# Block-sparse attention and a multiplicative FFN on one core: transposed scores in packed TensorE tiles, x kept on chip, w3 folded into w_out, the FFN interleaved with attention

## The chip, the cores and the metric

The kernel runs on one core of one Trainium2 chip. The metric is the device time of one execution in microseconds (us), as a median of several executions. Every run had runs of the kernel before as company on the same chip; the rounds ran on several chips, on which the kernel before had medians of 515.2 to 516.3 us, so times of different rounds are compared too. A run over 1.5% above the fastest of its kernel counts as slow, and verdicts use the others, called fast. Ratios are the mean time of one kernel's fast runs over that of the other's in the same rounds, so they are not quite the ratio of the medians.

Engines: PE is TensorE (matmuls; PEld is its weight load), ACT is ScalarE, DVE is VectorE, POOL is GpSimd, SP is SyncE. PSUM is the memory that matmuls write to.

## The reference, cut to what matters

```python
# q, k, v: (4 batches, 8 heads, 768 tokens, 64); blocks of 32 tokens
scores = q @ k.T / 8
mask   = near diagonal | first/last block row or column | 3 sampled blocks per block row
attn   = softmax(where(mask, scores, -1e9));  out = attn @ v
x = out.transpose(0, 2, 1, 3).reshape(3072, 512)     # heads side by side
a = x @ w1;  b = x @ w2                              # 512 -> 1024
h = (a * b) @ w3                                     # 1024 -> 1024
y = h @ w_out                                        # 1024 -> 512, float32
```

Nothing stands between `@ w3` and `@ w_out`, so `w3 @ w_out` can be formed once.

## The kernel before

Attention runs first, for each of 32 heads; x goes to DRAM in bf16; then the FFN reads it back transposed. The mask is part of the score matmul: Q and K carry 24 extra rows (64 + 24 = 88), which add -400 to masked scores. A column of ones in V gives the softmax sum.

```python
AUG = D + NB                                            # 88 rows
QTaugs = [aug_pool.tile([AUG, S], BF16, ...) for i in range(4)]
KTaugs = [aug_pool.tile([AUG, S], BF16, ...) for i in range(4)]
# ...
for c in range(NKC):                                    # 6 token chunks
    tq = tr_ps.tile([D, 128], BF16, tag="trq")
    nc.tensor.transpose(tq, qb16[:, c, :], ident)       # 64 rows of output
    nc.vector.tensor_copy(QTaug[:D, c * 128:(c + 1) * 128], tq)
    tk = tr_ps.tile([D, 128], BF16, tag="trq")
    nc.tensor.transpose(tk, kb16[:, c, :], ident)
    nc.vector.tensor_copy(KTaug[:D, c * 128:(c + 1) * 128], tk)
for kc in range(NKC):
    Sps = s_ps_pool.tile([128, S], F32, tag="sps")
    lhs = KTaug[:, kc * 128:(kc + 1) * 128]
    nc.tensor.matmul(Sps[:, 0:512], lhsT=lhs, rhs=QTaug[:, 0:512], start=True, stop=True)
    nc.tensor.matmul(Sps[:, 512:768], lhsT=lhs, rhs=QTaug[:, 512:768], start=True, stop=True)
    E = asb2.tile([128, S], BF16, tag="E")
    nc.scalar.activation(E, Sps, AF.Exp, scale=1.0 / 8.0)
    for qs in range(NKC):
        nc.tensor.matmul(Ops[:, qs, :], lhsT=E[:, qs * 128:(qs + 1) * 128],
                         rhs=Vaug[:, kc, :], ...)       # 65 columns
# ... normalize, nc.sync.dma_start(out=xd[b, h], in_=ox)
for t in range(NTT):                                    # FFN, 512 tokens each
    # xT by transposing DMA; pa = x w1, pb = x w2; hT = pa * pb
    # pg = hT w3 (384 matmuls in all); po = gT w_out; store
```

The softmax here doesn't subtract the row's maximum and nothing guards it: scores larger than these inputs give would overflow.

## Time and profile before

The median is 515.7 us. From the page of the profile: the span, the busy line, and of the 40 slices of the span the busy tenths of PE and ACT and the granted TensorE clock (PEclk), and the chain.

```profile
span 514.2 us, 7561 instructions
...
PE 490.2 (95%) x2880; PEld 223.7 (43%) x2880; DVE 138.2 (27%) x540; ACT 224.3 (44%) x313; POOL 50.8 (10%) x140
...
PE   2999999999999999999999579999999999999996
...
ACT  0465555555555555555464313333333333333332
...
PEclk9999999999999999999999999999999999999999
...
PE 95%; issue 1%; DMA 1%; DVE 1%; SPq 1%; POOL 1%; ACT 0%; POOLq 0%; ACTq 0%
```

The last line is the chain of work that ended last, by engine. PE is busy nearly all the time and is nearly all of the chain. That alone doesn't tell how fast it works. The PEclk row misleads here: the record of the granted clock has its first entry, full speed, at 305.6 us. Where there is no record yet, the page draws 9.

The timeline shows what the clock was. Columns: start (us), duration (us), engine, line, operation, output<-inputs, shapes, count. One iteration of attention:

```profile
152.33 0.51 PE L175 MATMUL Ops<-Vaug,E 128*128 128x65 bf16 x6
...
152.66 0.62 PE L168 MATMUL Sps<-QTaug_121,KTaug_125 88*128 88x512 bf16 x1
...
153.06 0.42 PE L170 MATMUL Sps<-QTaug_121,KTaug_125 88*128 88x256 bf16 x1
...
153.42 0.32 PE L157 MATMUL tq<-ident,qb_2218 128*64 128x128 bf16 x1
...
153.52 0.31 PE L160 MATMUL tk<-ident,kb_2219 128*64 128x128 bf16 x1
153.58 0.81 ACT L173 ACTIVATE E<-Sps 128x768 bf16<-128x768 f32 x1 [0.60 <-PE Sps L170]
```

The next Ops starts at 153.77: a period of 1.44 us. Read starts, not durations, since matmuls are pipelined. The 512-column score matmul keeps its successor back by 0.40 us here, 0.41 in the median of every stretch of attention. The 256 columns behind it should need 0.21 us, yet tq starts 0.35 us later: 0.14 us are lost where the output width changes. The chain that ended last (start, duration, what) shows the same matmul shape at both speeds at the beginning of the FFN:

```profile
301.51 1.71 PE pb L223 x4
303.21 1.71 PE pa L219 x4
304.92 1.27 PE pb L223 x4
306.19 0.86 PE pa L219 x4
...
316.55 13.81 PE pg L234 x64
```

Four 512-column matmuls take 1.71 us, then, after 4.7 us of uninterrupted work (from 300.9 us), 0.86 us, and 13.81 / 64 = 216 ns each from there on. So the whole attention stage ran at half the clock.

| Stage of the kernel before | From, to (us) | What sets it |
|---|---|---|
| Attention, 192 iterations | 13 to 291 | PE at half clock, 1.44 us an iteration |
| x to DRAM and back | 291 to 301 | DMA |
| FFN, 960 matmuls of 512 columns | 301 to 510 | PE at full clock, 216 ns each |

### The profile page before, as it was taken

To read this page: it belongs to the slowest core of one execution; us is meant where nothing else is said; L and a number is where in the kernel's file an instruction comes from. 1 tells how busy PE (TensorE), PEld (TensorE's weight loads), DVE (VectorE), ACT (ScalarE), POOL (GpSimd) and SP (SyncE) were. 2 spreads that over 40 slices of the span, in tenths; PEclk is the share of its full clock that TensorE was granted. 3 is DMA by queue.
4 is the path that set the end of the run, shared out by engine and by line. 5 is a ranking of instruction groups with operands and counts; after the bars stand their busy time and mean duration, and the time that the engine had idled before them with its cause. 6 is when DMAs were issued, how large, how long until landed. Compare 5 with 4: busy or idle time off the path is not lost.

```text
span 514.2 us, 7561 instructions
## 1 busy us (share of the span) xinstructions
PE 490.2 (95%) x2880; PEld 223.7 (43%) x2880; DVE 138.2 (27%) x540; ACT 224.3 (44%) x313; POOL 50.8 (10%) x140
## 2 busy tenths in 40 slices
PE   2999999999999999999999579999999999999996
PEld 1444444444444444444444224444444444444442
DVE  3323233333333323235554312021030130210300
ACT  0465555555555555555464313333333333333332
POOL 5221121212121212121100000000000000000000
PEclk9999999999999999999999999999999999999999
DMA  7453444444545353546554332111101200201002
GB/s 136 92 119 78 86 96 98 93 100 88 106 85 108 79 115 78 116 113 203 183 172 138 98 82 31 30 64 41 61 22 41 83 23 20 82 1 55 28 0 82
DMA packets 120681, 42.74 MB, mean 83 GB/s; under 512 B 114308, under 2 KB 114500, under 8 KB 120644
## 3 DMA queue, kind: packets, MB, share of 16 engines
q1 hardware_dynamic: 120644, 42.25, 34.2%
q8 instruction: 22, 0.36, 0.3%
q14 instruction: 15, 0.12, 0.1%
HBM read 29.36 MB, written 9.44 MB: 75 GB/s over the span
## 4 chain that ended last, share of the span: by engine, by line
PE 95%; issue 1%; DMA 1%; DVE 1%; SPq 1%; POOL 1%; ACT 0%; POOLq 0%; ACTq 0%
PE Ops L175 17%; PE pg L234 16%; PE Sps L168 16%; PE pb L223 8%; PE pa L219 8%; PE po L243 8%; PE Sps L170 8%; PE tq L157 8%; PE tk L160 5%; SPq L209 1%; DMA xT<-x_dram 1%; DMA x_dram<-ox 0%; ACT E L173 0%; DVE KTaug_125 L161 0%; DVE QTaug_122 L158 0%
## 5 line engine op out<-in xcount | busy, mean ns | idle before, releaser
L173 ACT ACTIVATE E<-Sps 128x768 bf16<-128x768 f32 x192 | 152.7, 810 | 135.9 <-PE Sps L170 133.4
L175 PE MATMUL Ops<-Vaug,E 128*128 128x65 bf16 x1152 | 98.5, 243 | 1.2 <-ACT E L173 1.2
L175 PEld LDWEIGHTS <-E 128*128 128x128 bf16 x1152 | 68.2, 126 | 38.2 <-issue 24.1
L234 PE MATMUL pg<-hT,w3sb 128*128 128x512 bf16 x384 | 83.9, 379 | 0.0
L228 DVE TENSOR_TENSOR hT<-pa_sb,pb 128x512 bf16<-128x512 bf16 x48 | 33.0, 688 | 164.4 <-PE pb L223 153.6
L219 PE MATMUL pa<-xT,w1sb 128*128 128x512 bf16 x192 | 51.5, 389 | 8.0 <-issue 5.8
L234 PEld LDWEIGHTS <-w3sb 128*128 128x128 bf16 x384 | 37.6, 98 | 45.3
L227 ACT CAST pa_sb<-pa 128x512 bf16<-128x512 f32 x48 | 28.1, 586 | 62.3 <-PE pa L219 62.3
L238 ACT CAST gT<-pg 128x512 bf16<-128x512 f32 x48 | 28.1, 586 | 59.9 <-PE pg L234 59.9
L223 PE MATMUL pb<-xT,w2sb 128*128 128x512 bf16 x192 | 50.6, 387 | 0.0
L243 PE MATMUL po<-woutsb,gT 128*128 128x512 bf16 x192 | 42.4, 379 | 0.0
L219 PEld LDWEIGHTS <-w1sb 128*128 128x128 bf16 x192 | 19.0, 99 | 31.2 <-issue 9.4
L223 PEld LDWEIGHTS <-w2sb 128*128 128x128 bf16 x192 | 19.1, 100 | 24.8 <-issue 3.1
L168 PE MATMUL Sps<-QTaug_122,KTaug_126 88*128 88x512 bf16 x48 | 29.7, 620 | 0.0
L168 PE MATMUL Sps<-QTaug_121,KTaug_125 88*128 88x512 bf16 x48 | 29.7, 619 | 0.0
L168 PE MATMUL Sps<-QTaug_123,KTaug_127 88*128 88x512 bf16 x48 | 29.7, 619 | 0.0
L168 PE MATMUL Sps<-QTaug_124,KTaug_128 88*128 88x512 bf16 x48 | 29.7, 619 | 0.0
L243 PEld LDWEIGHTS <-gT 128*128 128x128 bf16 x192 | 18.8, 98 | 22.7
L248 ACT COPY osb<-po 128x512 f32<-128x512 f32 x24 | 14.1, 586 | 27.4 <-PE po L243 27.4
L144 POOL CAST Vaug<-vf 128x384 bf16<-128x384 f32 x32 | 16.3, 510 | 58.3 <-issue 30.3
L170 PE MATMUL Sps<-QTaug_122,KTaug_126 88*128 88x256 bf16 x48 | 20.1, 418 | 0.0
L170 PE MATMUL Sps<-QTaug_121,KTaug_125 88*128 88x256 bf16 x48 | 19.9, 419 | 0.0
(244 smaller groups left out, 426.9 us busy)
## 6 DMA issues: line engine op xcount, KB each, us to landing
scratch<-in_moe_w_dram SPq DMA_DIRECT2D x16, 512.0 KB
qf<-in_q_dram SPq DMA_DIRECT2D x32, 192.0 KB
kf<-in_k_dram SPq DMA_DIRECT2D x32, 192.0 KB
vf<-in_v_dram SPq DMA_DIRECT2D x32, 192.0 KB
out_dram<-osb SPq DMA_DIRECT2D x24, 256.0 KB
x_dram<-ox SPq DMA_DIRECT2D x32, 96.0 KB
scratch<-in_moe_w_out_dram SPq DMA_DIRECT2D x8, 256.0 KB
xT<-x_dram SPq DMA_TRANSPOSE x24
```

The source lines that it names most:

```text
L157: nc.tensor.transpose(tq, qb16[:, c, :], ident)
L168: nc.tensor.matmul(Sps[:, 0:512], lhsT=lhs, rhs=QTaug[:, 0:512], start=True, stop=True)
L170: nc.tensor.matmul(Sps[:, 512:768], lhsT=lhs, rhs=QTaug[:, 512:768], start=True, stop=True)
L173: nc.scalar.activation(E, Sps, AF.Exp, scale=1.0 / 8.0)
L175: nc.tensor.matmul(Ops[:, qs, :], lhsT=E[:, qs * 128:(qs + 1) * 128], rhs=Vaug[:, kc, :], start=(kc == 0 and qs == 0), stop=(kc == NKC - 1 ...
L219: nc.tensor.matmul(pa, lhsT=w1_sb[:, dmc, fft * 128:(fft + 1) * 128], rhs=xT[:, dmc, :], start=(dmc == 0), stop=(dmc == NDMC - 1))
L223: nc.tensor.matmul(pb, lhsT=w2_sb[:, dmc, fft * 128:(fft + 1) * 128], rhs=xT[:, dmc, :], start=(dmc == 0), stop=(dmc == NDMC - 1))
L227: nc.scalar.copy(pa_sb, pa)
L228: nc.vector.tensor_mul(hT[:, fft, :], pa_sb, pb)
L234: nc.tensor.matmul(pg, lhsT=w3_sb[:, ffc, ff2t * 128:(ff2t + 1) * 128], rhs=hT[:, ffc, :], start=(ffc == 0), stop=(ffc == NFFC - 1))
L238: nc.scalar.copy(gT[:, ff2t, :], pg)
L243: nc.tensor.matmul(po, lhsT=gT[:, ff2c, tsub * 128:(tsub + 1) * 128], rhs=wout_sb[:, ff2c, :], start=(ff2c == 0), stop=(ff2c == NFFC - 1))
```

## The change

The kernel was rebuilt around TensorE:

- Scores come out with keys on partitions. Two heads share the array: each contracts over 64 rows, one in rows 0 to 63, one in rows 64 to 127.
- Values: the output has 32 channels on partitions, so four matmuls fit side by side in four column quarters. Softmax sums come from a matmul with ones.
- The mask is a bf16 multiplication on DVE after the exp.
- x stays on chip, already transposed. `w3 @ w_out` is formed once ("fold").
- FFN work is cut into pieces of four matmuls, which wait in a list and are popped between the matmuls of attention. There are 72 groups, each of two score blocks (2 heads, 256 queries, 256 keys) and the values of the group before.

The diff replaces nearly the whole body; its core:

```diff
-    lhs = KTaug[:, kc * 128:(kc + 1) * 128]
-    nc.tensor.matmul(Sps[:, 0:512], lhsT=lhs, rhs=QTaug[:, 0:512], ...)
-    nc.tensor.matmul(Sps[:, 512:768], lhsT=lhs, rhs=QTaug[:, 512:768], ...)
-    nc.scalar.activation(E, Sps, AF.Exp, scale=1.0 / 8.0)
+    for k2 in range(2):                       # scores(): one of two blocks of a group
+        kc = 2 * kp + k2
+        for h in range(2):
+            nc.tensor.matmul(s[:, h, k2 * QT:(k2 + 1) * QT],
+                             lhsT=qk[64 * h:64 * h + 64, 1, kc * 128:(kc + 1) * 128],
+                             rhs=qk[64 * h:64 * h + 64, 0, t * QT:(t + 1) * QT], ...)
+    nc.scalar.activation(e, s, AF.Exp, scale=1.0 / 8.0)
+    nc.vector.tensor_tensor(e, e, mask[...].to_broadcast((128, 2, 512)), op=ALU.mult)
 # ...
-    for qs in range(NKC):
-        nc.tensor.matmul(Ops[:, qs, :], lhsT=E[:, qs * 128:(qs + 1) * 128], rhs=Vaug[:, kc, :], ...)
+    for part in range(3):                     # values()
+        for g in range(4):                    # column quarter
+            rows = slice(32 * g, 32 * g + 32)
+            if part == 2:
+                nc.tensor.matmul(d[rows, :], lhsT=ones, rhs=rhs, ...)
+            else:
+                nc.tensor.matmul(o[rows, part * QT:(part + 1) * QT],
+                                 lhsT=vn[...][:, h, kc, 32 * part:32 * part + 32], rhs=rhs, ...)
 # ...
-    nc.tensor.matmul(pg, lhsT=w3_sb[...], rhs=hT[:, ffc, :], ...)    # for every token
+    nc.tensor.matmul(box["p"], lhsT=w3t_sb[...], rhs=wo_sb[:, j, :], ...)   # once: 64 matmuls
 # ...
+    for s, g in enumerate(groups):
+        # ... loads and transposes for later groups
+        n = 0 if s < 7 else (3 if s < 18 else 2)
+        scores(b, t, Q, kp, 0)
+        pop(n // 2)                           # FFN or fold pieces
+        scores(b, t, Q, kp, 1)
+        if prev is not None:
+            values(*prev)
+            finish(prev)
+        pop(n - n // 2)
+        prev = g
```

## The prediction

> **What bounds it now.** The windows view has PE busy 95% of 514 us, in two stages. Attention (to 291 us): the timeline repeats every 1.44 us, 192 times, 276 us. FFN (301 to 510 us): 960 matmuls of 512 columns, one every 216 ns. Between them about 10 us of waiting for x (x_dram store, transposing load). ScalarE (224 us) and VectorE (138 us) are not bounds.
>
> In attention PE is slow rather than merely busy. Single instructions of the trace: a 512-column score matmul holds its successor for 409 ns, against 216 ns in the FFN; the first FFN matmuls come every 427 ns and drop to 216 at 305.6 us, where the granted-clock record begins (the page's 9s before that are a default). So all attention runs at half clock. The Trainium skill, "TensorE: Matmul & The Clock Gate", Part 1, says the clock doubles after some 3.4 us of sustained activity; this trace agrees (4.5 us of dense FFN). Each change of output width (128 to 64 rows and back, for transposes) also shows about 0.13 us of nothing; the skill's "TensorEngine Tiling", Key Properties, says a mode change drains TensorE, and the trace fits.
>
> **Removed.** w3 product: 384 of 960 FFN matmuls, 83 us at 216 ns. The x round trip (10 us). Value matmuls of 65 columns with 128-wide weights. The 24 mask rows of K (88 to 64, so two heads share the rows).
>
> **Added.** Fold: 64 matmuls, 14 us, and 64 transposes, about 4 us. VectorE masks each exp: 144 of 128x1024 bf16; estimated 0.65 us each (a 512-column one with PSUM took 0.69), 94 us, hidden. 1728 small value matmuls, four side by side. Five or so mode changes in each of 72 groups.
>
> **Per group (warm), estimates from 216 ns per 512 columns.** Scores 4 slots of 256 columns: 0.45 us. Values 6 slots: 0.66 if four quarters really overlap, 1.5 if issue or weight loads bind; I take 1.0. Two FFN items: 1.73. Mode changes: 0.5. Transposes: 0.3. PE 4.0 us, against ScalarE 2.4 (two exps at 0.91, scaled from the 0.70 pitch of 768 columns; copies 0.59) and VectorE 2.5. PE remains the bound.
>
> **Sum.** First loads and transposes 14; groups 0-6 at cold clock 18; groups 7-17 with the fold 39, plus about 13 waiting for w3 (9 MB lie ahead of its end in the queue); 54 groups x 4.0 = 216; about 34 FFN items left at the end, 30, dense; last store 3. Total 333; most doubts (mode changes, overlap, w3 wait) can also come out better, so I say 320.
>
> **Critical path.** Nearly all PE work before and after; about 83 us of the gain is the fold, the rest mostly the doubled clock in attention, packing and the lost round trip.
>
> **Right if:** 512-column matmuls are 379 ns long (warm) nearly throughout and the granted clock is at full from about 40 us; groups 18-71 take 3.5-4.3 us; the chain of waits is over 80% PE; value matmuls start about 27-45 ns apart; PE busy alone at the end for about 30 us. **Wrong if:** the interleaved small matmuls and drains keep the clock low (groups then 6 us, total near 450); quarters run one after another (group 5 us, 370); ScalarE or VectorE turn out to be what PE waits for; or the loads through the GpSimd queue are slow and the early groups starve (+30).
>
> Predicted 320 us, range 280 to 385; faster by over 2%: 0.97, within 2%: 0.01, slower: 0.02.

## The result, and the profile after

The median is 306.84 us (306.75 to 307.35, 4 runs) against 515.69 us; the ratio of fast runs is 0.595 (95% interval 0.5939 to 0.5962). The same parts of the page, with the first line of the chain that ended last:

```profile
span 305.1 us, 7802 instructions
...
PE 282.8 (93%) x3412; PEld 129.2 (42%) x3412; DVE 188.1 (62%) x303; ACT 194.1 (64%) x250; POOL 48.0 (16%) x78
...
PE   0677787999999999999999999999999999999994
...
ACT  1198875544778866777777787568777777831310
...
PE 85%; ACT 6%; DVE 3%; POOL 2%; DMA 2%; issue 1%; ACTq 0%; POOLq 0%
```

PE is as busy as before, in 209 us less. ACT and DVE are now used throughout, and still don't bind. The granted clock is full from 24.9 us to the end. The windows view over groups 18 to 71 (busy time of each engine, with counts; then the clock, the DMA share and GB/s) has no idle PE at all (the modelled ends of matmuls cover the short losses read below):

```profile
80.30:267.90 187.60, 187.60 (x2355) 80.89 (x2355) 123.82 (x188) 141.95 (x182) 10.01 (x14) 1.00 0.17 39
```

One plain group in the timeline, PE only:

```profile
150.57 0.39 PE L181 MATMUL s<-qkt 64*128 64x256 bf16 x4
150.89 1.04 PE L291 MATMUL po<-wf_sb,h 128*128 128x512 bf16 x4
151.86 0.39 PE L181 MATMUL s<-qkt 64*128 64x256 bf16 x4
152.19 0.40 PE L211 MATMUL o<-e,vn 128*32 128x256 bf16 x8
152.41 0.28 PE L208 MATMUL d<-e,ones 128*32 128x256 bf16 x4
152.52 0.39 PE L211 MATMUL o<-e,vn 128*32 128x256 bf16 x8
152.74 0.28 PE L208 MATMUL d<-e,ones 128*32 128x256 bf16 x4
```

The group starts at 150.57 and its last FFN piece at 152.96; the next group starts at 153.93. That is a period of 3.36 us. Starts of the single matmuls within it: the two of a row-packed pair 3 ns apart, the four of a column-packed slot 3 ns apart, slots 109 ns apart. So both kinds of packing overlap fully: 24 value matmuls take 0.65 us. From the last FFN matmul to the first score matmul there are 312 ns, where the FFN's own pitch is 216: 96 ns are lost. The other four changes of tile shape in a group lose 90 to 96 ns each.

The predicted sum against the measured stages, from the starts of the score matmuls:

| Stage | Predicted (us) | Measured (us) |
|---|---|---|
| Until the first scores | 14 | 19.2 |
| Groups 0 to 6 | 18 | 17.2 |
| Groups 7 to 17, fold, wait for w3 | 39 + 13 | 43.9 |
| Groups 18 to 71 | 54 x 4.0 = 216 | 187.6, or 54 x 3.47 |
| FFN pieces left | 30 | 33.0 |
| Last store | 3 | 4.1 |

### The profile page after: what moved, and what is told of

It is laid out like the page before. It is cut to its first block, busy times and chain, and to the rows that moved or that the text cites. A ratio compares the mean times of both kernels' runs of the same rounds, so it can differ in the third digit from the quotient of the medians.

```text
span 305.1 us, 7802 instructions
## 1 busy us (share of the span) xinstructions
PE 282.8 (93%) x3412; PEld 129.2 (42%) x3412; DVE 188.1 (62%) x303; ACT 194.1 (64%) x250; POOL 48.0 (16%) x78
## 3 DMA queue, kind: packets, MB, share of 16 engines
q0 software_dynamic: 16416, 14.68, 31.2%
## 4 chain that ended last, share of the span: by engine, by line
PE 85%; ACT 6%; DVE 3%; POOL 2%; DMA 2%; issue 1%; ACTq 0%; POOLq 0%
PE pb L281 15%; PE po L291 15%; PE pa L270 15%; PE s L181 14%; PE o L211 12%; PE wp L252 5%; PE d L208 5%; ACT e L186 4%; PE tp L167 3%; DMA kn<-in_k_dram 2%; DVE e L187 1%; ACT mask L157 1%; PE mp L155 1%; PE w3p L239 1%; DVE w3t_sb L241 1%
## 5 line engine op out<-in xcount | busy, mean ns | idle before, releaser
L186 ACT ACTIVATE e<-s 128x1024 bf16<-128x1024 f32 x144 | 146.7, 1025 | 47.5 <-PE s L181 42.1
L187 DVE TENSOR_TENSOR e<-e,mask 128x1024 bf16<-128x1024 bf16 x144 | 99.4, 690 | 79.2 <-ACT e L186 79.0
L181 PE MATMUL s<-qkt 64*128 64x256 bf16 x576 | 57.3, 280 | 3.7 <-ACT e L186 2.3
L211 PE MATMUL o<-e,vn 128*32 128x256 bf16 x1152 | 54.0, 277 | 1.3 <-DVE x L227 1.1
L281 PE MATMUL pb<-x,w_sb 128*128 128x512 bf16 x192 | 49.6, 381 | 0.4 <-DVE h L283 0.4
L270 PE MATMUL pa<-x,w_sb 128*128 128x512 bf16 x192 | 49.7, 381 | 0.0
L291 PE MATMUL po<-wf_sb,h 128*128 128x512 bf16 x192 | 47.3, 381 | 0.0
L208 PE MATMUL d<-e,ones 128*32 128x256 bf16 x576 | 41.8, 275 | 0.0
L181 PEld LDWEIGHTS <-qkt 64*128 64x128 bf16 x576 | 17.6, 95 | 54.4 <-issue 51.5
L283 DVE TENSOR_TENSOR h<-pb,a 128x512 bf16<-128x512 f32 x48 | 32.9, 685 | 10.7 <-PE pb L281 10.7
L211 PEld LDWEIGHTS <-vn 128*32 128x32 bf16 x1152 | 25.2, 96 | 18.0 <-issue 17.2
L281 PEld LDWEIGHTS <-w_sb 128*128 128x128 bf16 x192 | 15.5, 97 | 23.4 <-issue 11.0
L270 PEld LDWEIGHTS <-w_sb 128*128 128x128 bf16 x192 | 15.7, 98 | 21.7 <-issue 8.0
L227 DVE TENSOR_TENSOR x<-o,rec 128x512 bf16<-128x512 f32 x24 | 16.6, 692 | 2.2 <-ACT rec L226 1.8
## 6 DMA issues: line engine op xcount, KB each, us to landing
w_sb<-in_moe_w_dram POOLq DMA_DIRECT2D x1, 2048.0 KB, 16.9
```

The costliest lines, as they stand in the source:

```text
L181: nc.tensor.matmul(s[:, h, k2 * QT:(k2 + 1) * QT], lhsT=qk[64 * h:64 * h + 64, 1, kc * 128:(kc + 1) * 128], rhs=qk[64 * h:64 * h + 64, 0, ...
L186: nc.scalar.activation(e, s, AF.Exp, scale=1.0 / 8.0)
L187: nc.vector.tensor_tensor(e, e, mask[:, t, kp:kp + 1, :].to_broadcast((128, 2, 512)), op=ALU.mult)
L208: nc.tensor.matmul(d[rows, :], lhsT=ones, rhs=rhs, start=first, stop=last, skip_group_check=True)
L211: nc.tensor.matmul(o[rows, part * QT:(part + 1) * QT], lhsT=vn[b, 2 * Q + i][:, h, kc, 32 * part:32 * part + 32], rhs=rhs, start=first and ...
L270: nc.tensor.matmul(p, lhsT=w1_sb[:, c, f * 128:(f + 1) * 128], rhs=x[:, c, :], start=c == 0, stop=c == 3)
```

## The experiments

Twelve runs follow, each of another kernel; all gave correct results. Two questions led them. Which parts of the change carry the 209 us? And why did the kernel before run at half clock for 300 us, when the changed one left it after 25?

### FFN after attention instead of inside it

```diff
-        n = 0 if s < 7 else (3 if s < 18 else 2)
+        n = 0
-    xpool = pool("xpool", 3)
+    xpool = pool("xpool", 6)
```

> The changed kernel with the fold and the whole FFN put after attention instead of between its matmuls (same matmuls, same order otherwise). Theory (TensorE is the bound only because the FFN is there to fill it; attention alone is bound by ScalarE at two exps of 0.92 us plus a third of ln and exp, about 2.2 us a group, and the clock stays full as it did in groups 2 to 6): attention 72 x 2.2 = 158 us, then 18 us of fold and 6 x 21.9 us of FFN, in all about 333 us. Rival (the dense FFN matmuls are what keeps the clock up): matmuls in attention go back to half clock, groups of 2.6 us or more, over 355 us.

Measured: 354.91 us, 48 us more than the changed kernel. That is at the edge of the rival's range, but by the theory's mechanism: the granted clock was full from 24.8 us to the end, so dense FFN work isn't what holds it up. Groups without transposes took 2.16 us on average, ScalarE's pace, as the theory has it. Groups that also carry transposes took up to 3.3 us, which the theory had left out. Interleaving is worth 48 us because it fills TensorE's waits for ScalarE. The windows view of a stretch of attention without transposes (the columns as above) has ScalarE (ACT, the fourth) busy for 23.40 of 24 us and PE for 18.19:

```profile
66.00:90.00 24.00, 18.19 (x354) 10.62 (x352) 17.99 (x26) 23.40 (x31) 1.43 (x2) 1.00 0.15 21
```

### The kernel before, with zero rows

```diff
-    QTaugs = [aug_pool.tile([AUG, S], BF16, ...)        # 88 rows; KTaugs alike
+    QTaugs = [aug_pool.tile([128, S], BF16, ...)
+        nc.gpsimd.memset(QTaugs[i][64:128, :], 0.0)     # before the 24 mask rows are loaded
+        nc.gpsimd.memset(KTaugs[i][64:128, :], 0.0)
```

> The kernel before with the augmented Q and K padded from 88 to 128 rows by zeros: same instruction count and columns[...]. Theory A (what keeps the clock at half in attention is idle time and mode changes, 0.27 us of each 1.44): nothing changes, 516 us. Theory B (the unused rows count as idle): clock goes full in attention, period limited by ScalarE near 0.9 us, about 415 us.

Measured: 427.38 us (425.2 to 427.85), ratio 0.8278. Forty rows of zeros, which change no result and no column count, took 88 us off. The clock record is full from 22.4 us (to 203.3, where the FFN waits for x, and again from 213.6). The same iteration in its timeline, PE only:

```profile
100.17 0.36 PE L177 MATMUL Ops<-Vaug,E 128*128 128x65 bf16 x6
...
100.36 0.38 PE L170 MATMUL Sps<-QTaug,KTaug 128*128 128x512 bf16 x1
...
100.58 0.27 PE L172 MATMUL Sps<-QTaug,KTaug 128*128 128x256 bf16 x1
...
100.78 0.24 PE L159 MATMUL tq<-ident,qb 128*64 128x128 bf16 x1
```

The score matmul keeps its successor back by 0.22 us, not 0.40. The exps now follow each other every 0.96 us on average over the stage, instead of 1.45. Theory B's number, 415, was 3% low. The mode changes and waits of theory A are still there, and didn't stop the clock.

### The kernel before, with one wide transpose

```diff
-    qb16 = asb.tile([128, NKC, D], ...); kb16 = asb.tile([128, NKC, D], ...)
+    qk16 = asb.tile([128, NKC, 2, D], BF16, tag="qk16")       # q and k side by side
-    nc.tensor.transpose(tq, qb16[:, c, :], ident)             # 64 rows out, twice
-    nc.tensor.transpose(tk, kb16[:, c, :], ident)
+    tqk = tr_ps.tile([128, 128], BF16, tag="trq")
+    nc.tensor.transpose(tqk, qk16[:, c].rearrange("p a d -> p (a d)"), ident)
+    nc.vector.tensor_copy(QTaug[:D, ...], tqk[:D, :]);  nc.vector.tensor_copy(KTaug[:D, ...], tqk[D:, :])
```

> The kernel before with one 128-wide transpose of q and k together instead of two 64-wide ones: one transpose of 128 columns less and no change of output width, so none of the two 0.13 us gaps in each iteration. Theory A (gaps and transposes keep the clock down): TensorE has no idle time left at half clock, the clock goes full, period limited by ScalarE near 0.9 us, total about 410 us. Theory B (something else keeps it at half clock, such as 88 of 128 rows): period 1.11 us from the half-clock pitches, about 452 us.

Measured: 408.96 us (407.56 to 410.54), ratio 0.792. Here 88 rows stayed, and the clock was full from 21.1 us (to 178.1, where the FFN waits for x, and again from 202.0). So neither of the two theories is right alone: taking away the gaps together with one transpose is enough, and so is filling the rows. Whether the gaps or the transpose counted, no run separates. Both edits raise the work that the array does in a stretch of time; that this is what counts, and that the kernel before lies just under a threshold, is a guess so far.

### The kernel before, with 96 rows

> The kernel before with the augmented Q and K padded from 88 to 96 rows only[...]. Theory (activity is counted in row strips or anything that does not see the last 8 rows, or the threshold lies well above): attention stays at half clock, 516 us, while 128 rows gave 427. Rival (the kernel before lies just below the threshold, so a little more activity is enough): about 427 us.

The edit is that of the 128 rows, with 96 in place of 128. Measured: 430.04, 520.21, 435.88 and 520.64 us in four runs. The two runs of about 520 count as slow, so the ratio 0.8383 is of the other two: 96 rows can bring the full clock. The profiled run was the one of 430 us; its iterations took 1.43 us, as in the kernel before, until the clock was full at 31.9 us. The 520 us runs weren't profiled; that their clock stayed at half in attention is inferred from their times, which are those of the kernel before, and from their mean recorded clock, 0.999 like its own (0.984 in the two fast runs: there the clock is on record from early on, and falls back while the FFN waits for x). With 88 rows the kernel before never left 514.8 to 517.5 us, with 128 rows it stayed at 425 to 428. A kernel at a threshold would look like this, and it agrees with the rival; four runs, two of them slow, don't show it. An estimate from the shapes and the half-clock periods in the traces (1.43 us an iteration, 1.07 with one wide transpose): rows x columns x streamed columns of all matmuls, per us, are 12.0 million for the kernel before, 12.5 with 96 rows, 14.7 with 128 rows, 16.0 with one transpose. A threshold near 12.5 would fit all four. How the chip counts the activity, and where the threshold lies in its units, stays open.

### The w3 product for every token

The fold is removed; the product with w3 becomes 16 more pieces per 512 tokens, evicted by DVE, and the last product uses w_out.

```diff
+        for f in range(NF):
+            fill.append(pg(f, 0));  fill.append(pg(f, 1))     # gT = (h w3), 4 matmuls each
-                    nc.tensor.matmul(box["o"], lhsT=hT[...], rhs=wf_sb[:, f, :], ...)
+                    nc.tensor.matmul(box["o"], lhsT=gT[...], rhs=wo_sb[:, f, :], ...)
-    for i in range(NF): fill.append(fold_transpose(i, 0)); ...; fill.extend(fold_mm(i))
```

> The changed kernel without the fold: the product with w3 is done for every token as before (384 matmuls of 512 columns more, evicted by VectorE), the 64 fold matmuls and 64 fold transposes are gone. Theory (TensorE bound nearly throughout): 83 us more, 17 us less for the fold, and a few us less of waiting in groups 7 to 17, which become bound by ScalarE: 365 to 375 us. Rival (part of the extra work hides in time that TensorE now waits): under 350 us.

Measured: 378.66 us, 72 us more. This is a little over the expected range and far from the rival's: TensorE's work is the time. The prediction's own arithmetic for the fold (83 less 14 and 4) gives 65. Of the 18 us for the fold only 8 came back: groups 7 to 17 took 35.7 us instead of 43.9.

### Scores on the whole array, twice

K of each head goes into a tile whose other 64 rows are zero, so the score matmuls contract over 128 rows one after the other.

```diff
-                                 lhsT=qk[64 * h:64 * h + 64, 1, kc * 128:(kc + 1) * 128],
-                                 rhs=qk[64 * h:64 * h + 64, 0, t * QT:(t + 1) * QT],
+                                 lhsT=z[:, h, kc * 128:(kc + 1) * 128],
+                                 rhs=qk[:, t * QT:(t + 1) * QT],
```

> The changed kernel with scores on the whole array: K of each head is stored in a tile whose other 64 rows are zero, so a score matmul contracts over 128 rows and two heads no longer run side by side. Theory (the row halves save 0.40 us of streaming a group but cost three of the five mode changes, 0.29 us): only about 0.12 us a group more, 8 us in all, 315 us. Rival (row packing is worth the streaming that it halves): 0.40 us a group, 336 us.

Measured: 332.22 us, near the rival's number, but for another reason: the memsets of the zero halves stood ahead of the loads in GpSimd's order, and the first scores came at 29.0 us instead of 19.2. The zeroing was moved to VectorE and the run repeated.

> Scores on the whole array again, with the zero halves written by VectorE when it is idle instead of by GpSimd ahead of the loads, which delayed the first scores by 10 us. Theory (row halves and mode changes nearly cancel): steady groups at 3.48 as in the earlier run, first scores near 20 us, total about 320 us with the extra copies of K in groups with transposes. Rival (the loss of 25 us was the doubled streaming): still 330 us.

Measured: 324.77 us, 18 us more than the changed kernel, between the two. The first scores come at 19.3 us. Plain groups take 3.48 us against 3.36, the 0.12 us of the theory: in its trace there is no gap between FFN and scores in either direction, only around the values. Over groups 18 to 71 the loss is 10.5 us (285.7 less 87.6, against 187.6). About half of it is 46 plain groups at 0.12 us; the rest sits in the eight with transposes and the groups next to them, which need more copies of K. The other 7 us are lost before group 18. So packing two heads into the rows gains little in a plain group, because it makes the scores a tile shape of their own between FFN pieces.

### Quarters one after another

```diff
-            for part in range(3):
-                for g in range(4):
+            for g in range(4):
+                for part in range(3):
```

> The changed kernel with the 12 value matmuls of a key block issued quarter by quarter (three for quarter 0, then three for quarter 1, and so on) instead of going round the quarters: same instructions. Theory (four matmuls share a slot of 109 ns only if they stand next to each other on different column quarters): nine slots instead of three a block, 1.3 us more a group, about 395 us. Rival (the queue overlaps them in any order): 307 us.

Measured: 308.76 us, 0.6% more. The theory fell. The program now issues output, output, sum for quarter 0, then for quarter 1, and so on. The timeline:

```profile
149.97 0.42 PE L211 MATMUL o<-e,vn 128*32 128x256 bf16 x8
150.20 0.30 PE L208 MATMUL d<-e,ones 128*32 128x256 bf16 x4
150.31 0.41 PE L211 MATMUL o<-e,vn 128*32 128x256 bf16 x8
150.52 0.30 PE L208 MATMUL d<-e,ones 128*32 128x256 bf16 x4
```

Eight output matmuls come first and four sums after them, as if the program had gone round the quarters. In this trace the four quarters start 10 ns apart and then each proceeds at 109 ns a matmul. So the order among quarters needn't be arranged by hand over a stretch of twelve matmuls. This says nothing of what column packing is worth; no run took it away.

### Fewer mode changes, first attempt

```diff
         scores(b, t, Q, kp, 0)
-        pop(n // 2)
         scores(b, t, Q, kp, 1)
         if prev is not None:
             values(*prev);  finish(prev)
-        pop(n - n // 2)
+        pop(n)
```

> The changed kernel with both score blocks of a group issued together and the FFN pieces of the group put in one place, after the value matmuls: three mode changes a group instead of five, nothing else changed. Theory (each change of the array's mode costs about 95 ns of TensorE time that nothing hides): 2 x 0.095 x about 60 groups = 11 to 12 us less, about 295 us. Rival (the gaps are waits that would appear elsewhere, or ScalarE is starved by the other order): within 2% of 307 us.

Measured: 314.92 us, 8 us worse. From group 18 on groups took 3.15, 3.15 and 3.49 us in turn: the two mode changes of 0.1 us are gone, but every third group waits. In the timeline of such a group (one with a short wait, 3.33 us):

```profile
120.26 0.69 DVE L227 TENSOR_TENSOR x<-o,rec 128x512 bf16<-128x512 f32 x1
120.27 0.61 PE L181 MATMUL s<-qkt 64*128 64x256 bf16 x8
...
121.00 0.40 PE L211 MATMUL o<-e,vn 128*32 128x256 bf16 x8
```

The values overwrite the one accumulator that the normalization (L227) still reads until 120.95. Groups with transposes reached 4.8 us (4.15 in the changed kernel), since the second scores wait for DVE's copy of the transposed heads, which no FFN piece now hides; and the fold's three transposes stand together and wait for DVE. By size the fold is nearly all of the loss: groups 7 to 17 took 50.5 us instead of 43.9, while from group 18 on the gains and the waits cancel within 0.5 us.

### Fewer mode changes, second attempt

From group 18 on: both score blocks, both FFN pieces, the transposes if there are any, then the values.

```diff
         scores(b, t, Q, kp, 0)
+        if s < 18: pop(n // 2)
         scores(b, t, Q, kp, 1)
+        if s >= 18:
+            pop(n)
+            if tr is not None: transposes(b + 1, tr)
         values(*prev);  finish(prev)
+        if s < 18: pop(n - n // 2)
```

> The changed kernel with three blocks a group from group 18 on: both score blocks, then both FFN pieces, then the values (with the transposes of the next batch just before the values); groups before 18 as they were. Theory (the run with one FFN block lost its gain because the values of the next head group came too soon after the normalization, because transposes stood between scores and their buffers, and in the fold; the mode change itself is real at 95 ns): plain groups at 3.15 us instead of 3.36, every third one too, and groups with transposes at about 3.9 instead of 4.15: 0.21 x 54 = 11 us less, 296 us. Rival (what is taken from mode changes comes back as waits whatever the order): 305 us or more.

Measured: 299.38 us (299.15 to 299.65), ratio 0.5807 to before, against 0.595: 2.4% faster than the changed kernel. All plain groups take 3.15 us. One in the timeline, PE only, from its scores to those of the next group:

```profile
106.11 0.61 PE L181 MATMUL s<-qkt 64*128 64x256 bf16 x8
106.65 1.90 PE L291 MATMUL po<-wf_sb,h 128*128 128x512 bf16 x8
108.48 0.40 PE L211 MATMUL o<-e,vn 128*32 128x256 bf16 x8
...
109.25 0.61 PE L181 MATMUL s<-qkt 64*128 64x256 bf16 x8
```

Groups with transposes and their neighbours (3.94, 4.40, 3.55 against 4.15, 4.15, 3.36) gained nothing, so 7.5 us came of the 11 expected. A mode change of 95 ns is real time when TensorE is the bound; how much of it is kept depends on which buffer the new order makes it wait for.

### More on top: masks, last pieces

> The run of three blocks plus two things: only the mask of the first token block is built before the first scores (the others in groups 1 and 3, copies mostly on VectorE), and FFN pieces after the last group use the scores' PSUM buffers too. Expected on top of the three blocks: 3 to 4 us from the mask, about 1 us from the last pieces (0.14 us of waiting for each of 9 pairs): 291 us. If the first loads set the start instead, the mask gives nothing and it is 295 us.

The edit builds only the first mask before the first scores and lets the pieces after the last group use two more PSUM buffers. Measured: 299.02 us, but with a spread of 296.72 to 300.98: the same as the run before it within its noise. In the profiled run (296.72 us) the first scores came at 14.5 us instead of 19.3, yet group 6 starts at 33.5, against 34.3. The masks made TensorE wait in groups 0 and 2, and the clock fell back from 25.7 to 29.1 us. The fallback isn't what makes the spread: the two faster runs (296.7 and 297.5 us) have a mean recorded clock of 0.994, as this fallback gives, and the two near 301 have 1.0; these weren't profiled, so the spread stays unexplained. The pieces at the end gave their 2 us (31.2 instead of 33).

### More on top: transposes in other buffers

> The run of three blocks, with the transposes from group 18 on written to the FFN's PSUM buffers (q and k apart, just before the FFN pieces) instead of the scores' buffers, and with FFN pieces after the last group using the scores' buffers too; the masks as in the changed kernel. Expected: groups with transposes 0.8 us over the plain 3.15 instead of 1.2 on average (5 us less over 12 pairs) and 1.8 us less at the end as the earlier run showed: 293 us. If the transposes wait for VectorE's copies in any buffer: 298 us.

```diff
+            tp = ps_f.tile([128, 1024], BF16, tag="f", name="tw")    # q, then k
...
         if s >= 18:
+            if tr is not None: transposes_two(b + 1, tr)
             pop(n)
```

Measured: 319.42 us, 20 us worse than three blocks. The timeline shows the mistake and its price, in the first group with transposes and at the end of the same wait in the next:

```profile
118.88 0.53 PE L179 MATMUL tw<-ident,qn 128*64 128x128 bf16 x12
...
119.24 0.50 PE L179 MATMUL tw<-ident,kn 128*64 128x128 bf16 x12
...
120.75 0.69 DVE L198 TENSOR_TENSOR e<-e,mask 128x1024 bf16<-128x1024 bf16 x1 [0.23 <-ACT e L197]
121.36 1.02 DVE L181 COPY qkt<-tw 128x768 bf16<-128x768 bf16 x2
121.96 0.50 PE L301 MATMUL pb<-x,w_sb 128*128 128x512 bf16 x1 [2.22 <-DVE qkt L181]
...
122.68 1.06 PE L301 MATMUL pb<-x,w_sb 128*128 128x512 bf16 x2 [0.22 <-issue]
...
130.21 1.02 PE L301 MATMUL pb<-x,w_sb 128*128 128x512 bf16 x3 [2.63 <-DVE qkt L181]
```

DVE took its work in the order of the program: its copy of the transposes (L181) stood behind both masks (L198), which wait for both exps, so the FFN piece that needs the buffer waited 2.22 us. Then the clock went to half for 3.4 us (the record: half from 122.1 to 125.5), and the next 512-column matmuls came 0.43 us apart. That group took 7.84 us; a plain one takes 3.15. All eight groups with transposes had such a wait, of 2.2 to 3.0 us, and took 6.2 to 7.9 us, so the waits are most of the loss. The clock fell to half at three of them (122.1, 139.1 and 200.6 us), not at the other five, among them the longest. After waits of the same length, a group with the fall took 1.3 to 1.6 us more than one without. Each wait stood behind transposes; whether these count less for the clock than other matmuls, no run shows.

## Why the prediction was right or wrong, point by point

- **Direction, size and range: right.** 306.8 us lies in 280 to 385. Its point, 320, was 4% high, and its sum, 333, was 9% high.
- **"All attention runs at half clock" before, and full clock after: right.** The run with zero rows shows what the clock alone was worth in the old structure: 88 us (the 107 us of the run with one wide transpose contain a transpose and the gaps as well). The prediction named sustained activity as what frees the clock, and drains as what might keep it low in the new kernel. That is incomplete: unfilled rows count too, as the padded runs show. Which property of the new kernel frees its clock was not taken apart, beyond that the FFN isn't needed for it.
- **The per-group sum of 4.0 us: the mis-sized step.** It measured 3.47 us on average. The values were put at 1.0 us, between 0.66 "if four quarters really overlap" and 1.5 "if issue or weight loads bind"; they took 0.65, so the quarters overlap. Transposes were put at 0.3 us a group; groups with them took 0.79 us more, but only 8 of these 54 had any, which makes 0.12. Five mode changes were put at 0.5 us and took about 0.47. These explain 0.56 us a group, as good as the whole 0.53.
- **The wait of 13 us for w3: wrong.** The load of w3 was issued at 13.1 us and landed 16.9 us later, at 30.0, before group 7 (36.3 us) needed it. In its place the fold's groups ran slower than put down, 44 us instead of 39.
- **Groups 0 to 6: 17.2 us against 18, by luck.** They were put at the cold clock, but it was full from 24.9 us, in group 2. Groups 3 to 6, at full clock, took 2.67 us on average, no less than groups 0 to 2 (2.16), so the match doesn't come from the cold clock.
- **Start: too low by 5 us.** The nine mask copies, which take turns between PE and ACT from 13.6 to 19.2 us, weren't counted.
- **ScalarE and VectorE not the bound: right.** In groups 18 to 71 they were busy 142 and 124 of 187.6 us, 2.63 and 2.29 us a group, against the estimates of 2.4 and 2.5. The mask took 690 ns for 1024 bf16 elements (estimate 0.65 us). The Trainium skill, "VectorE: DVE Perf Modes", the perf-mode tier table, allows bf16 `tensor_tensor` in SBUF twice the base rate; the trace agrees, with 512 elements from PSUM at 685 ns and 1024 from SBUF at 690 ns.
- **The signs named in advance:** 512-column matmuls 381 ns long on average; clock full from 24.9 us (named: about 40); the chain 85% PE (named: over 80%); value matmuls 27 ns apart on average, as four at once every 109 ns (named: 27 to 45); 33 us of FFN at the end (named: about 30).
- **Shares of the gain: partly right.** Without the fold the changed kernel takes 72 us more, against the 83 that "about 83 us of the gain is the fold" names and the 65 net of its costs. Interleaving, 48 us, was not sized at all; it stood hidden in the assumption that PE has no idle time. Row packing, named among the causes, is worth 18 us at most. The parts don't add up exactly, since each was taken alone, and no run took away column packing or put x back in DRAM.

## What to carry to other kernels

When PE shows busy 95%, look at the spacing of like matmuls before believing it: a stage at half clock looks just as busy, and here rows of zeros, or one transpose and its gaps less, brought the full clock. When TensorE is the bound, fill its waits for other engines with independent matmuls, and gather matmuls of one tile shape, but check for each new order which single buffer, or which in-order queue behind a copy, it makes TensorE wait for. Waits of 2 to 3 us cost their own length, and three of eight were followed by 3.4 us at half clock as well.

## What the Trainium skill lacked or had wrong

- "TensorE: Matmul & The Clock Gate", Part 1, speaks of sustained matmul activity as what frees the clock. It lacks that rows used count: with the same matmuls, 88 rows never got full clock in attention (514.8 to 517.5 us), 96 rows in two of four runs (430 and 436 us; the other two 520), 128 rows in all (425 to 428 us).
- The same page's table "Why this matters for your kernels" warns of idle gaps over about 3 us. Here eight waits of 2.2 to 3.0 us stood behind transposes: three (2.22, 2.22 and 2.62 us) were followed by half clock for 3.4 us, and the longest, 2.96 us, was not. So within this span the length of the gap alone didn't decide it.
- "TensorEngine Tiling (Array Packing)", Key Properties, says that a mode change drains TensorE, but gives no time: it was 90 to 96 ns at full clock and about 137 ns at half clock (351 ns behind 256 columns, against 214 without the change). Going from FFN matmuls to scores over 128 rows, the same tile shape, cost nothing, while going to scores in row halves cost 96 ns.
- "TensorE: Matmul & The Clock Gate", Part 3, "The mechanism", has matmuls start in strict program order. In the run with quarters in turn, the trace shows matmuls of different column quarters starting out of program order, 10 ns apart, and the time changed by 0.6% only.
- The caveats in Part 1 of the clock page call recorded clock events unreliable. Here the recorded changes agree with the spacing of the matmuls (427 to 216 ns around 305.6 us); what misled was the time before the first record, which no page mentions and which a profile draws as full speed.
